# Gated delta rule feeding a folded four-matrix FFN on one core: the first five chunks' work cut into one-engine steps and issued from a single list

## The chip, the cores and the metric

The kernel runs on one core of a Trainium2 chip. The metric is the device time of one execution in microseconds (us). The core has a matrix engine (TensorE, PE in the profile, with its weight loads as PEld), a vector engine (VectorE, DVE), a scalar engine (ScalarE, ACT), a general engine (GpSimd, POOL) and a sequencer that issues DMAs (SyncE, SP). Each engine takes its instructions strictly in the order in which they were written into its queue.

## The reference

For 4 batches and 8 heads, a 48x48 state is carried over 768 tokens; then a multiplicative FFN is applied to the result.

```python
k_n = k / (np.linalg.norm(k, axis=-1, keepdims=True) + 1e-06)
for t in range(S):
    kt, vt, bt = (k_n[:, :, t], v[:, :, t], beta[:, :, t, None])
    y[:, :, t] = np.einsum('bhd,bhde->bhe', q[:, :, t], state)
    v_old = np.einsum('bhde,bhd->bhe', state, kt)
    state = state + bt[:, :, :, None] * np.einsum('bhd,bhe->bhde', kt, vt - v_old)
...
x = np.ascontiguousarray(attn_out.transpose(0, 2, 1, 3)).reshape(B * S, H * D)
a = x @ w1
b = x @ w2
h = a * b @ w3
return (h @ w_out).astype(np.float32)
```

q, k, v and beta are float32; w1, w2 (384x1024), w3 (1024x1024) and w_out (1024x384) arrive as float64.

## The kernel before

**The recurrence.** The 768 tokens are cut into 12 chunks of 64. For chunk m: `scores(m)` multiplies K by (K, Q) on TensorE and leaves U (scaled, DVE) and PT (masked). U goes to DRAM in 32x32 blocks (`to_blocks`), and for each pair of chunks j `inverse(j)` loads it back as Ub and solves 31 dependent steps on DVE, two operations each (L304, L309). The result Vb goes through DRAM into TT (`from_blocks`); `corner(m)` completes the 64x64 inverse on TensorE, and `chain(m)` does the three products with the state S and the outputs, which ACT copies into xT, the FFN's input.

**The weights.** All float64 weights come in 36 pieces: 8 of w_out (384 KB each), 16 of w3 and 12 of w1 and w2 (512 KB each). A piece is loaded into one of five `raw` buffers and converted (`convert`) by two ACT operations (L470, L471), two DVE operations (L473, L476) and one POOL addition (L479). A buffer is free for the next load when the POOL addition is done; the load of the next piece is written right after it (`converts`). The w3 pieces are transposed on TensorE (L514), and w3 times w_out is computed once, in eight parts (`fold(jc)`, L521, each in two halves), as w34. w_out lies in the space of w2, so w2 can't be converted before the last fold.

**The FFN.** For every pair of chunks u: eight `ab` units (L543, three matmuls with w1 and three with w2, then ACT's copy and DVE's product) and four `o` units (L558, eight matmuls with w34 and the store).

**The order.** Up to half of the second inverse the order is written out by hand, and `in_text_order` ties every engine to it; behind that point (`tc.issue_after`) a scheduler orders the rest by priority and readiness, from the same text order. In the hand-written part a `convert` issues all of its ACT, DVE and POOL operations at one place, and a `transpose_w3` and a `fold` follow the two conversions that they need.

Of the kernel before, what the change touches and what calls it, by code (L numbers as in the profile page):

```python
# [30 lines left out]

@with_exitstack
def kernel(
# [46 lines left out]
    turns = {}  # L82
# [71 lines left out]
    def load_k(m, dma):  # L154
        ktoks[m] = load_tok(k, m, dma, "ktok", 4)

    def load_v(m, dma):
        vtoks[m] = load_tok(v, m, dma, "vtok", 2)

    def load_perm(m, dma):  # L160
        for src, dst in ((k, kperm), (q, qperm)):
            for z in range(2):
                for j in range(2):
                    nd = min(BS, D - BS * j)
                    for tb in range(2):
                        t0 = C * m + BS * tb
                        dma(  # L167
# [6 lines left out]
                        )  # L174

# [6 lines left out]
    def squares(j):  # L182
        sums[j] = ss = small.tile([P, 2, NR, H], FP32, name="ss")
        for cc in range(2):
            kt = ktoks[2 * j + cc]
            for r in range(NR):
                sq = in_turn(work, [P, H, D], "sq", 1, "sq")
                pool.tensor_tensor(out=sq[:], in0=kt[:, r], in1=kt[:, r], op=ALU.mult)
                dve.tensor_reduce(out=ss[:, cc, r], in_=sq[:], axis=AX.X, op=ALU.add)
                yield  # L190
    def norms(j):
        ss = sums.pop(j)
        seed = small.tile([P, 2, NR, H], U32, name="seed")
# [5 lines left out]
        for _ in range(3):  # L199
            t = small.tile([P, 2, NR, H], FP32, name="nt", bufs=3)  # L200
# [4 lines left out]
            rn = small.tile([P, 2, NR, H], FP32, name="nr", bufs=3)  # L205
# [14 lines left out]
        ns[j], ws[j] = n, w  # L220

# [29 lines left out]
    def scores(m, transposed=None):  # L251
        Us[m] = U = in_turn(work, [P, NR, H, C], "U", 2, "U")
        PTs[m] = PT = in_turn(work, [P, NR, H, C], "PT", 3, "PT")
        w = scale_of(ws, m)
        for r in range(NR):
            if transposed:
                transposed(m, r)
            KQ = KQs[m, r]
            ps = two_banks()
            for h in range(H):  # L260
                for z in range(2):
# [5 lines left out]
                    )  # L267
            psv = ps[:].rearrange("p a (h j t) -> p (a h) j t", h=4, j=2)
            dve.tensor_tensor(  # L269
                out=U[:, r], in0=psv[:, :, 0, :],  # L270
                in1=w[:, r].unsqueeze(2).to_broadcast([P, H, C]), op=ALU.mult,
            )
            dve.tensor_tensor(
                out=PT[:, r], in0=psv[:, :, 1, :],
                in1=smask[:].unsqueeze(1).to_broadcast([P, H, C]), op=ALU.mult,
            )
# [6 lines left out]
    def to_blocks(m, dma):  # L283
        j = m // 2
        if m % 2 == 0:
            Uds[j] = dram.tile([P, BS, BS], FP32, tag="Ud", name="Ud")
        for x in range(4):
            dma(
                out=Uds[j][:].rearrange(blocks, x=4, r=NR, h=H)[m % 2, x],
                in_=Us[m][quarter(x), :, :, quarter(x % 2)].rearrange("s r h t -> s (r h) t"),  # L290
            )

    def inverse(j, dma):
        U = work.tile([P, BS, BS], FP32, tag="Ub", name="Ub", bufs=1)
# [16 lines left out]
        Vds[j] = dram.tile([P, BS, BS], FP32, tag="Vd", name="Vd")  # L311
        dma(out=Vds[j][:], in_=V[:])

    def from_blocks(m, dma):
        for x in range(4):
            dma(
                out=TTs[m % 2][quarter(x), :, :, quarter(x % 2)].rearrange("s r h t -> s (r h) t"),
                in_=Vds[m // 2][:].rearrange(blocks, x=4, r=NR, h=H)[m % 2, x],
            )


    def corner(m):
        TT, U = TTs[m % 2], Us.pop(m)
# [6 lines left out]
        ps = psT.tile([P, NR, H, BS], FP32, tag="t", name="ps_t")  # L330
        for r in range(NR):
            for h in range(H):
                for z in range(2):
                    pe.matmul(  # L334
                        ps[quarter(2 * z + 1), r, h, :], lhsT=U[quarter(2 * z), r, h, BS:C],
                        rhs=T11[quarter(2 * z), r, h, :], start=True, stop=True,
                    )
        for z in range(2):
# [3 lines left out]
        ps = psT.tile([P, NR, H, BS], FP32, tag="t", name="ps_t")  # L342
        for r in range(NR):
            for h in range(H):
                for z in range(2):
# [12 lines left out]
    def chain(c):  # L358
        w = scale_of(ws, c)
        TT, PT, kt = TTs[c % 2], PTs.pop(c), ktoks.pop(c)  # L360
        KQ = [KQs.pop((c, r)) for r in range(NR)]
        nv = vtoks.pop(c)
        for r in range(NR):
# [3 lines left out]
            )  # L367

# [10 lines left out]
        if c == 0:  # L379
            R = nv  # L380
        else:
            R = work.tile([P, NR, H, D], FP32, tag="R", name="R", bufs=1)
            ps = products(
                lambda r, h, z: KQ[r][feat(z), h, 0, :], lambda r, h, z: St[feat(z), r, h, :], C
            )
            dve.tensor_tensor(out=R[:], in0=nv[:], in1=ps, op=ALU.subtract)
# [4 lines left out]
        X = in_turn(work, [P, NR, H, D], "X", 2, "X")  # L391
# [389 lines left out]
```

## Time and profile before

| | us |
|---|---|
| median of 3 runs (758.71 to 760.46) | 758.8 |
| the profiled execution's own time | 758.51 |
| its span (first to last instruction) | 756.8 |
| TensorE matmul busy in the span | 645.0 (85%) |
| VectorE, ScalarE, GpSimd busy | 351.8, 156.8, 97.5 |
| DMA moved in the span | 55.60 MB |

The span is what the engines' records cover; 1.7 us lie around it. Busy time of TensorE counts a matmul longer when the granted clock is low, so a busy engine is not one that works at full speed. The first FFN matmul starts at 215.64 us of the span.

### The profile page before, as it was taken

What the parts mean: (1) busy time and instruction counts of PE and PEld (TensorE: products, weight loads), DVE (VectorE), ACT (ScalarE), POOL (GpSimd) and SP (SyncE); (2) the same over time, 40 slices, a digit from 0 to 9 for tenths busy, and PEclk for the clock granted to TensorE, in tenths of its full rate; (3) what the DMA queues carried; (4) which work ended last, traced back from release to release, by engine and by line L of the source; (5) the groups of instructions that cost most, each with busy time, mean ns of one, the idle gap of its engine ahead of it and who ended that gap; (6) DMA issues with size and microseconds to landing.
All of it is one profiled execution on the core that took longest, in us unless ns stands there. A gap on an engine that the chain in (4) does not pass through costs nothing.

```text
span 756.8 us, 17007 instructions
## 1 busy us (share of the span) xinstructions
PE 645.0 (85%) x7372; PEld 400.3 (53%) x7372; DVE 351.8 (46%) x768; ACT 156.8 (21%) x277; POOL 97.5 (13%) x110
## 2 busy tenths in 40 slices
PE   5524577578848999879998999999999999999998
PEld 5512334466613367644667547575476645655444
DVE  2877532331468923478325862369442492200110
ACT  3522223322242022010210113111130112211010
POOL 4331221211154100021000100002000000000000
PEclk9756677675779999999999999999999999999999
DMA  9584551151289053451433432334413402000001
GB/s 193 142 207 128 108 133 56 44 97 29 55 180 127 1 91 54 110 83 34 62 64 86 93 65 36 69 84 83 86 22 55 96 11 57 3 22 32 0 1 42
DMA packets 201834, 55.60 MB, mean 73 GB/s; under 512 B 191968, under 2 KB 195040, under 8 KB 201760
## 3 DMA queue, kind: packets, MB, share of 16 engines
q1 hardware_dynamic: 197600, 53.74, 34.6%
q10 hardware_dynamic: 4160, 0.79, 0.7%
q8 instruction: 58, 0.95, 0.5%
q14 instruction: 16, 0.13, 0.1%
HBM read 42.30 MB, written 11.01 MB: 70 GB/s over the span
## 4 chain that ended last, share of the span: by engine, by line
PE 66%; DVE 13%; issue 4%; DMA 3%; SPq 2%; POOL 2%; ACT 1%; POOLq 0%; DVEq 0%; ACTq 0%
PE ps_f L543 24%; PE ps_f L558 15%; PE ps_w L375 7%; PE ps_w L262 6%; PE ps_f L521 6%; DVE Vb L309 4%; DVE tb L304 4%; PE ps_t L347 2%; PE ps_t L334 2%; DMA raw<-in_moe_w_dram 1%; PE ps_w L425 1%; PE ps_w L420 1%; SPq L167 1%; PE ps_f L514 1%; POOL w L479 1%
## 5 line engine op out<-in xcount | busy, mean ns | idle before, releaser
L543 PE MATMUL ps_f<-xT,w1s 128*128 128x512 f32 x288 | 138.8, 614 | 16.5 <-DMA xT<-xT 11.2
L543 PE MATMUL ps_f<-xT,w2s 128*128 128x512 f32 x288 | 135.3, 601 | 4.8 <-POOL w2s L479 3.9
L558 PE MATMUL ps_f<-w,ab 128*128 128x384 f32 x384 | 128.3, 490 | 0.0
L543 PEld LDWEIGHTS ps_f<-xT,w1s 128*128 128x128 f32 x288 | 54.2, 195 | 83.7 <-issue 60.3
L558 PEld LDWEIGHTS ps_f<-w,ab 128*128 128x128 f32 x384 | 71.9, 190 | 49.6 <-issue 3.0
L543 PEld LDWEIGHTS ps_f<-xT,w2s 128*128 128x128 f32 x288 | 53.8, 191 | 70.1 <-issue 62.1
L553 DVE TENSOR_TENSOR ab<-a,ps_f 128x512 f32<-128x512 f32 x48 | 32.8, 683 | 122.5 <-PE ps_f L543 122.4
L304 DVE TENSOR_TENSOR tb<-Vb,Ub 128x31 f32<-128x31 f32 (+15 forms) x186 | 72.8, 392 | 9.4 <-DMA Ub<-Ud 4.9
L309 DVE TENSOR_TENSOR Vb<-Vb,tb 128x31 f32<-128x31 f32 (+15 forms) x186 | 72.4, 389 | 4.7
L262 PE MATMUL ps_w<-KQ 48*64 48x128 f32 x768 | 57.2, 314 | 16.3 <-DVE KQ L234 11.4
L550 ACT COPY a<-ps_f 128x512 f32<-128x512 f32 x48 | 28.0, 586 | 205.2 <-PE ps_f L543 205.1
L262 PEld LDWEIGHTS ps_w<-KQ 48*64 48x64 f32 x768 | 52.9, 159 | 19.8 <-issue 15.2
L514 PE MATMUL ps_f<-ident,w 128*128 128x128 f32 x64 | 17.3, 424 | 52.3 <-POOL w L479 52.3
L521 PE MATMUL ps_f<-w2s,w3T 128*128 128x384 f32 x128 | 55.4, 593 | 0.0
L364 POOL TENSOR_TENSOR vtok<-vtok,n 128x384 f32<-128x384 f32 x24 | 19.8, 849 | 226.3 <-DMA vtok<-in_v_dram 166.6
L269 DVE TENSOR_TENSOR U<-ps_w,w 128x512 f32<-128x512 f32 x24 | 16.5, 686 | 66.5 <-PE ps_w L262 66.5
L436 ACT COPY xT<-ps_w 48x512 f32<-48x512 f32 x48 | 27.9, 580 | 76.7 <-PE ps_w L425 76.2
L514 PEld LDWEIGHTS ps_f<-ident,w 128*128 128x128 f32 x64 | 11.2, 212 | 58.9 <-POOL w L479 58.6
L521 PEld LDWEIGHTS ps_f<-w2s,w3T 128*128 128x128 f32 x128 | 29.5, 240 | 20.6 <-issue 10.8
L563 ACT COPY osb<-ps_f 128x384 f32<-128x384 f32 x24 | 11.5, 479 | 126.6 <-PE ps_f L558 116.2
L479 POOL TENSOR_TENSOR w<-w,raw 128x512 uint32<-128x512 uint32 x16 | 20.7, 1291 | 116.7 <-DVE w L476 106.1
L393 DVE TENSOR_TENSOR X<-ps_w,w 128x384 f32<-128x384 f32 x24 | 12.3, 553 | 42.5 <-PE ps_w L375 42.5
(78 smaller groups left out, 628.6 us busy)
## 6 DMA issues: line engine op xcount, KB each, us to landing
raw<-in_moe_w_dram SPq DMA_DIRECT2D x16, 512.0 KB, 5.0
vtok<-in_v_dram SPq DMA_DIRECT2D x24, 192.0 KB, 4.0
raw<-in_moe_w_dram SPq DMA_DIRECT2D x24, 192.0 KB, 4.1
out_dram<-osb SPq DMA_DIRECT2D x24, 192.0 KB, 1.9
ktok<-in_k_dram SPq DMA_DIRECT2D x22, 192.0 KB, 4.5
raw<-in_moe_w_out_dram SPq DMA_DIRECT2D x8, 384.0 KB, 6.4
Ud<-U SPq DMA_DIRECT2D x48, 64.0 KB, 1.9
Ub<-Ud SPq DMA_DIRECT2D x6, 512.0 KB, 4.6
```

Of the source, the lines that this page charges most:

```text
L262: pe.matmul(ps[half(z), h // 4, 128 * (h % 4) : 128 * (h % 4) + 128], lhsT=KQ[feat(z), h, 0, :], rhs=KQ[feat(z), h].rearrange("p j t -> p ...
L304: dve.tensor_tensor(out=tv, in0=V[:, 0 : s + 1, s : s + 1].to_broadcast([P, s + 1, n]), in1=U[:, s, s + 1 : BS].unsqueeze(1).to_broadcast( ...
L309: dve.tensor_tensor(out=o, in0=o, in1=tv, op=ALU.subtract)
L375: pe.matmul(o, lhsT=lhs(r, h, z), rhs=rhs(r, h, z), start=True, stop=True)
L436: act.copy(out=xT[f, :, NR * z : NR * z + NR, cc, :].rearrange("p a r t -> p r a t"), in_=pyv[f, z],)
L479: pool.tensor_tensor(out=au, in0=au, in1=lo, op=ALU.add)
L514: pe.transpose(ps[:, x, :], w3[:, x * P : (x + 1) * P], ident[:])
L521: pe.matmul(ps[:, 0:DM], lhsT=w3Ts[jc, kc // 4][:, kc % 4 * P : kc % 4 * P + P], rhs=wo[:, kc], start=(kc == 0), stop=(kc == KF - 1),)
L543: pe.matmul(ps[:], lhsT=w[:, m, js], rhs=cur["x"][:, m].rearrange("p b c t -> p (b c t)"), start=(m == 0), stop=(m == KM - 1),)
L550: act.copy(out=a[:], in_=pair[0][:])
L553: dve.tensor_tensor(out=t[:], in0=a[:], in1=pair[1][:], op=ALU.mult)
L558: pe.matmul(ps[:, 0:DM], lhsT=cur["ab"][jc][:, b * P : (b + 1) * P], rhs=w34[:, jc, :], start=(jc == 0), stop=(jc == KF - 1),)
```

## The change

All parts (`scores`, `inverse`, `corner`, `chain`, the new `outputs` and `scaled_v`, `piece` in place of `load_weight` and `convert`, `transpose_w3`, `fold`, `ab`, `o`, the loads) become generators that yield after the work of each single engine. A string of 551 names, `ORDER`, says which part takes its next step; it ends behind the fourth chunk's outputs, the sixth chunk's scores (s5) and the whole third inverse. The tail behind it is as before, from chunk 4 on. In the names, P0 to P7 are w_out pieces, P8 to P23 w3 pieces, P24 to P29 w1, P30 to P35 w2; t is a transposition of a w3 piece, f a fold, s scores, u to_blocks, V an inverse, e a corner, n the scaled v, c a chain, y outputs, a0x a unit `ab`, o0x a unit `o`, k, q, v, p loads, K and Q transposed k and q, g and N the norms.

Beside the order, three things change: the first inverse (V0) works in PSUM, in one of the two two-bank buffers, which is held for it (`held`), with ACT copying in and out; PT of the first two chunks is copied by ACT and masked by POOL in place of one DVE operation; and q, k, v, w_out and w3 pieces are loaded in another order.

```diff
+ORDER = """
+P10 P2 k0 K00 g0 q0 P2 P2 P2 P10 P10 P10 K01 g0 g0 K00 P1 P1 k1 K10 P1 beta K01 K01 K00 beta
...
     def in_turn(pool, shape, tag, n, name, dt=FP32):
 
-        i = turns[tag] = (turns.get(tag, -1) + 1) % n
-        return pool.tile(shape, dt, tag=f"{tag}{i}", name=name, bufs=1)
+        i = turns.get(tag, -1)
+        while True:
+            i = turns[tag] = (i + 1) % n
+            if (tag, i) not in held:
+                return pool.tile(shape, dt, tag=f"{tag}{i}", name=name, bufs=1)
...
+            if m < 2:
+                act.copy(out=PT, in_=psv[:, :, 1, :])
+                yield
+                pool.tensor_tensor(out=PT, in0=PT, in1=mask, op=ALU.mult)
+            else:
+                dve.tensor_tensor(out=PT, in0=psv[:, :, 1, :], in1=mask, op=ALU.mult)
+            yield
...
+        V = Vb
+        if j == 0:
+
+            V = two_banks().rearrange("p a (s t) -> p (a s) t", t=BS)
+            held.add(("w", turns["w"]))
+            for i in range(0, BS, BS // 2):
+                act.copy(out=V[:, i : i + BS // 2], in_=Vb[:, i : i + BS // 2])
+                yield
...
+        if j == 0:
+            for i in range(0, BS, BS // 2):
+                act.copy(out=Vb[:, i : i + BS // 2], in_=V[:, i : i + BS // 2])
+                yield
+            held.clear()
...
-    def convert():
-        dst, raw = pieces.pop(0)
+        yield
         dst = dst()
-        n = dst.shape[1]
         lo, hi = raw[:, 0:n, 0], raw[:, 0:n, 1]
+        du = dst.bitcast(U32)
 
         act.activation(out=dst, in_=hi.bitcast(FP32), func=ACTF.Abs, scale=2.0**-112)
         act.activation(out=lo, in_=lo, func=ACTF.Copy, scale=2.0**-29)
...
+        yield
+        dve.tensor_scalar(out=du, in0=du, scalar1=3, scalar2=None, op0=ALU.logical_shift_left)
+        dve.scalar_tensor_tensor(
+            out=du, in0=hi, scalar=0x80000000, in1=du, op0=ALU.bitwise_and, op1=ALU.bitwise_or
         )
...
+        yield
+        pool.tensor_tensor(out=du, in0=du, in1=lo, op=ALU.add)
+        yield
...
+    for name in ORDER.split():
+        step(name)
     in_text_order()
```

What this does to three queues is shown as the rows of the built programs, before and after. TensorE between the second chunk's scores and the second fold, before (L514 transposes a w3 piece, L521 is a fold; x8 is a whole fold, x4 half of one):

```order
L262 MATMUL ps_w<-KQ 64x128 x64
L514 MATMUL ps_f<-ident,w_487 128x128 x4
L514 MATMUL ps_f<-ident,w_495 128x128 x4
L514 MATMUL ps_f<-ident,w_526 128x128 x4
L514 MATMUL ps_f<-ident,w_552 128x128 x4
L521 MATMUL ps_f<-w2s,w3T 128x384 x8
L514 MATMUL ps_f<-ident,w_602 128x128 x4
L514 MATMUL ps_f<-ident,w_628 128x128 x4
L521 MATMUL ps_f<-w2s,w3T 128x384 x8
```

and after (L578 transposes, L587 folds, L389 is the first corner's first product):

```order
L288 MATMUL ps_w<-KQ 64x128 x32
L578 MATMUL ps_f<-ident,w_140 128x128 x4
L578 MATMUL ps_f<-ident,w_450 128x128 x4
L578 MATMUL ps_f<-ident,w_217 128x128 x4
L578 MATMUL ps_f<-ident,w_503 128x128 x4
L578 MATMUL ps_f<-ident,w_526 128x128 x4
L578 MATMUL ps_f<-ident,w_495 128x128 x4
L587 MATMUL ps_f<-w2s,w3T 128x384 x16
L578 MATMUL ps_f<-ident,w_643 128x128 x4
L578 MATMUL ps_f<-ident,w_591 128x128 x4
L587 MATMUL ps_f<-w2s,w3T 128x384 x16
L578 MATMUL ps_f<-ident,w_706 128x128 x4
```

Six transpositions now stand ahead of the first fold, and folds follow each other two at a time with no transposition between them. On DVE, in the first inverse (tb and Vb steps are L304 and L309), each conversion of a w3 piece (L473, L476) stands before:

```order
L309 TENSOR_TENSOR Vb<-Vb,tb 128x12x20
L473 TENSOR_SCALAR w_602<-w_602 128x512
L476 SCALAR_TENSOR_TENSOR w_602<-raw,w_602 128x512
L304 TENSOR_TENSOR tb<-Vb,Ub 128x247
```

and the stretch of the same steps after (L350 and L355 are the steps, L538 and L539 the conversions; w2s at 384 columns is a w_out piece):

```order
L355 TENSOR_TENSOR ps_w<-ps_w,tb 128x10x22
L538 TENSOR_SCALAR w_591<-w_591 128x512
L539 SCALAR_TENSOR_TENSOR w_591<-raw,w_591 128x512
L538 TENSOR_SCALAR w2s<-w2s 128x384
L539 SCALAR_TENSOR_TENSOR w2s<-raw,w2s 128x384
L538 TENSOR_SCALAR w2s<-w2s 128x384
L539 SCALAR_TENSOR_TENSOR w2s<-raw,w2s 128x384
L538 TENSOR_SCALAR w2s<-w2s 128x384
L539 SCALAR_TENSOR_TENSOR w2s<-raw,w2s 128x384
L350 TENSOR_TENSOR tb<-ps_w,Ub 128x231
```

One w3 piece and the last three w_out pieces stand inside the inverse, which now reads and writes PSUM (ps_w). On SP, the DMA queue from the first inverse's input (Ub) on, before:

```order
L295 DMA Ub<-Ud 128x1024
L459 DMA raw<-in_moe_w_dram 128x1024 x3
L144 DMA ktok<-in_k_dram 64x16x48 x4
L144 DMA vtok<-in_v_dram 64x16x48 x2
L459 DMA raw<-in_moe_w_dram 128x1024 x4
L167 DMA kperm_96<-in_k_dram 32x16x32 x2
```

and after:

```order
L336 DMA Ub<-Ud 128x1024
L527 DMA raw<-in_moe_w_out_dram 128x768 x2
L527 DMA raw<-in_moe_w_dram 128x1024
L171 DMA ktok<-in_k_dram 64x16x48 x2
L527 DMA raw<-in_moe_w_out_dram 128x768 x2
L527 DMA raw<-in_moe_w_dram 128x1024
L527 DMA raw<-in_moe_w_dram 48x1024
```

Before, all w_out pieces were loaded ahead of Ub, and w1 came behind all of w3; now four w_out pieces follow Ub, six w3 pieces and one w1 piece stand ahead of it, and w1 pieces are mixed with w3 pieces.

## Rows read from the trace of the kernel before

**Rows 1.** Windows: length; busy PE, PEld, DVE, ACT, POOL; PEclk, DMA share, GB/s:

```profile
0.00:215.60 215.60, 131.55 (x1548) 98.32 (x1548) 102.69 (x201) 64.25 (x115) 52.52 (x60) 0.71 0.48 110
...
215.60:258.90 43.30, 35.73 (x73) 14.39 (x73) 33.26 (x69) 9.90 (x17) 15.87 (x15) 0.93 0.68 111
...
258.90:346.80 87.90, 78.09 (x1149) 51.37 (x1149) 47.00 (x111) 14.15 (x25) 8.46 (x10) 0.96 0.40 73
```

**Rows 2.** Who waited for whom: us in total, times, longest:

```profile
POOL w L479 <- DVE w L476: 106.1, 14, 18.9
...
PE ps_f L514 <- POOL w L479: 52.3, 14, 7.5
...
SPq L459 <- POOL w L479: 79.4, 10, 18.4
```

**Rows 3.** Timeline of TensorE: start, us, instruction, idle before it and its releaser:

```profile
73.34 1.11 PE L514 MATMUL ps_f<-ident,w 128*128 128x128 f32 x4 [6.25 <-POOL w L479]
...
74.25 7.52 PE L521 MATMUL ps_f<-w2s,w3T 128*128 128x384 f32 x16
...
215.64 4.29 PE L543 MATMUL ps_f<-xT,w1s 128*128 128x512 f32 x6 [7.31 <-DMA xT<-xT]
```

**Rows 4.** Two windows of 20 us, columns as in Rows 1:

```profile
0.00:20.00 20.00, 11.37 (x283) 10.82 (x285) 6.32 (x12) 8.28 (x14) 9.30 (x19) 1.00 0.92 184
...
40.00:60.00 20.00, 8.69 (x26) 5.58 (x27) 13.65 (x31) 4.56 (x8) 5.17 (x4) 0.55 0.88 205
```

**Rows 5.** Timeline of SP and DVE around the first inverse:

```profile
44.78 0.34 SPq L295 DMA_DIRECT2D Ub<-Ud  x1
...
48.07 0.77 DVE L304 TENSOR_TENSOR tb<-Vb,Ub 128x31 f32<-128x31 f32 x1 [0.69 <-DMA Ub<-Ud]
...
90.02 0.21 DVE L309 TENSOR_TENSOR Vb<-Vb,tb 128x31 f32<-128x31 f32 x1
...
97.73 4.04 SPq L316 DMA_DIRECT2D TT<-Vd  x8
```

**Rows 6.** Timeline of DVE and POOL, one conversion inside the first inverse:

```profile
68.51 0.42 DVE L309 TENSOR_TENSOR Vb<-Vb,tb 128x256 f32<-128x256 f32 x1
...
70.67 0.42 DVE L473 TENSOR_SCALAR w<-w 128x512 uint32<-128x512 uint32 x1
...
71.13 0.69 DVE L476 SCALAR_TENSOR_TENSOR w<-raw,w 128x512 uint32<-128x512 uint32 x1
...
71.95 1.33 POOL L479 TENSOR_TENSOR w<-w,raw 128x512 uint32<-128x512 uint32 x1 [6.04 <-issue]
...
72.18 1.38 DVE L309 TENSOR_TENSOR Vb<-Vb,tb 128x247 f32<-128x247 f32 x1
```

**Rows 7.** Groups of lines, 0 to 215.6 us: busy us, mean ns:

```profile
L309 DVE TENSOR_TENSOR Vb<-Vb,tb 128x31 f32<-128x31 f32 (+15 forms) x31 | 14.6, 471 | 1.1
...
L304 DVE TENSOR_TENSOR tb<-Vb,Ub 128x31 f32<-128x31 f32 (+15 forms) x31 | 11.1, 360 | 1.6 <-DMA Ub<-Ud 0.7
```

**Rows 8.** Groups of lines, whole span, two DVE operations that read PSUM:

```profile
L269 DVE TENSOR_TENSOR U<-ps_w,w 128x512 f32<-128x512 f32 x24 | 16.5, 686 | 66.5 <-PE ps_w L262 66.5
...
L393 DVE TENSOR_TENSOR X<-ps_w,w 128x384 f32<-128x384 f32 x24 | 12.3, 553 | 42.5 <-PE ps_w L375 42.5
```

**Rows 9.** DMA issues: KB each, median us to landing:

```profile
raw<-in_moe_w_dram SPq DMA_DIRECT2D x16, 512.0 KB, 5.0
...
TT<-Vd SPq DMA_DIRECT2D x48, 64.0 KB, 2.3
```

**Rows 10.** Chain that ended last, TensorE pieces at full clock: start, us, what:

```profile
363.35 1.13 PE ps_t L334 x64
...
398.79 3.64 PE ps_w L262 x64
...
405.77 2.00 PE ps_w L375 x64
...
732.46 20.65 PE ps_f L558 x64
```

More of the change, by code (lines that the diff above doesn't have):

```diff
@@ L367, in chain @@
             )
+            yield
+    def chain(c):
+        TT, nv = TTs[c % 2], vtoks[c]
+        KQ = [KQs[c, r] for r in range(NR)]
         def products(lhs, rhs, rows):
@@ L410, in chain, with outputs @@
             yield
+    def outputs(c):
+        PT, St, X = PTs[c], Ss.get(c), Xs[c]
+        KQ = [KQs[c, r] for r in range(NR)]
         py = two_banks()
@@ new lines, in ab, with o @@
+        yield
+    def o(u, b):
+        ps = bank([P, NT])
+        for jc in range(KF):
+            pe.matmul(
+                ps[:, 0:DM], lhsT=abs_[u, jc][:, b * P : (b + 1) * P], rhs=w34[:, jc, :],
+                start=(jc == 0), stop=(jc == KF - 1),
+            )
+        yield
+        osb = in_turn(ffn, [P, DM], "o", 2, "osb")
+        act.copy(out=osb[:], in_=ps[:, 0:DM])
+        yield
+        t0 = b * S + u * 2 * C
+        sync.dma_start(out=out[t0 : t0 + P, :], in_=osb[:])
+        yield
@@ L629 @@
-    norms(0)
-    for r in range(NR):
-        by_tensor(1, r, 1, qs[1])
-        converts(1)
-    for m in range(2):
-        first = scores(m)
-        for _ in range(2):
-            next(first)
-            converts(1)
-        to_blocks(m, sp)
-    V = inverse(0, sp)
-    next(V)
-    converts(3)
-    transpose_w3(0)
-    load_k(2, sp)
-    load_k(3, sp)
-    load_v(0, sp)
-    folds = [fold(jc) for jc in range(KF)]
-    corners = [corner(0), corner(1)]
-    chains = [chain(0), chain(1)]
-    later = [scores(2, by_vector), scores(3, by_vector)]
@@ L702 @@
[L702 to L715 removed]
+        yield
+        ps = bank([P, NCH, NR * H])
+        for c in range(NCH):
+            pe.transpose(
+                ps[:, c, :], beta_fm[:, c].rearrange("p z t -> p (z t)"),
+                ident[0 : 2 * H, 0 : 2 * H],
+            )
@@ new lines, in betas_ @@
+        yield
+        dve.tensor_copy(
+            out=beta_tok[:].rearrange("p c r h -> p c (r h)"), in_=ps[:, :, 0 : NR * H]
+        )
+        yield
+    parts = {"beta": betas_}
+    for m in range(NCH):
+        parts[f"k{m}"] = lambda m=m: load_k(m, act.dma_start if m == 0 else sync.dma_start)
+        parts[f"v{m}"] = lambda m=m: load_v(m)
+        parts[f"p{m}"] = lambda m=m: load_perm(m)
+        parts[f"s{m}"] = lambda m=m: scores(m)
+        parts[f"u{m}"] = lambda m=m: to_blocks(m)
+        parts[f"e{m}"] = lambda m=m: corner(m)
+        parts[f"n{m}"] = lambda m=m: scaled_v(m)
+        parts[f"c{m}"] = lambda m=m: chain(m)
+        parts[f"y{m}"] = lambda m=m: outputs(m)
@@ L716, with step, finish @@
+    running = {}
+    def step(name):
+        if name not in running:
+            running[name] = parts[name]()
+        next(running[name], None)
+    def finish(*names):
+        for name in names:
+            if name not in running:
+                running[name] = parts[name]()
+            for _ in running[name]:
+                pass
+    for name in ORDER.split():
+        step(name)
     in_text_order()
+    last = [i for i in nc.cur_bb.bb.instructions if i.engine == mybir.EngineType.SP][-1]
@@ L719, in emit @@
+    units = [f"a1{jc}" for jc in range(KF)] + [f"o1{b}" for b in range(B)]
     def emit(n):
[L720 to L739 removed]
+        finish(*units[:n])
+        del units[:n]
```

431 lines of the change are left out of this document (179 added, 252 removed).

## The prediction, made before the run

> **What bounds the kernel now.** I read four views: the windows for a cut into stages, the waits for what stands behind the idle time, the timelines for the pace of one conversion and of the first inverse, and the chain for full-clock prices. The windows [rows 1] show two kernels in one. Up to 215.6 us, where the first FFN matmul starts [rows 3], TensorE is busy 131.6 us at a mean granted clock of 0.71 and idle for 84; behind that it is nearly always busy: idle 7.6 of 43.3 and 9.8 of 87.9 us in the next two stretches. No other engine fills the front: DVE is busy 102.7, ACT 64.3, POOL 52.5 of 215.6 us, and DMA moves 110 GB/s, where it moved 184 and 205 in its best stretches [rows 4].
>
> So what bounds the front is a round trip. A w3 piece needs ACT, then DVE (0.42 + 0.69 us), then POOL (1.33) [rows 6], then TensorE, and the hand-written order issues the next piece behind the previous fold's copy and between steps of the inverse. The waits [rows 2] show each link: POOL waits 106.1 us for DVE's half of a conversion, TensorE 52.3 us for POOL's addition in front of its transpositions, and SP 79.4 us for POOL to free a load buffer. Each pause also costs speed: a fold of 16 records behind an idle 6.25 us took 7.52 us [rows 3], while at full clock (64 records of the same shape in 20.65 us, 0.323 each [rows 10]) it would be 5.16.
>
> **The change, part by part.** Nothing on TensorE is added or removed; the change moves the start of the FFN. I call that start F (215.6 before) and work out the new one, first along the engines, then by bytes.
>
> *First inverse, start.* DMA sizes follow from shapes: a w_out piece 0.393 MB, a w1, w2 or w3 piece 0.524 [rows 9], a q, k or v tile (64 tokens x 32 heads x 48 x 4 bytes) 0.393, U's blocks of one chunk 0.262, Ub, Vd or two chunks' TT 0.524. Ahead of Ub in the new queue stand six w3, one w1 and four w_out pieces, five q and k tiles, half a K/Q load (0.393), beta and U's blocks of two chunks: 8.22 MB. I take 190 GB/s, between the two best stretches and nearer the first, which has small rows: 43 us, plus 2.3 for the last blocks to land [rows 9], plus the 3.3 from Ub's issue to the first step before [rows 5]: 49 us, against 48.07. Nothing is won here, though four w_out pieces fewer are loaded by then.
>
> *First inverse, run.* It took 25.7 us of DVE time [rows 7], of which some 3.5 are steps that ran beside a POOL addition: 1.38 where a like step takes 0.42 [rows 6]. With V in PSUM I expect 2 x 11.1 = 22.2 us, 0.72 for each pair. Inside it now stand w_out pieces whose last (P7) comes 11.23 MB into the queue: 59 + 2.3 = 61.4, ACT's part about 1.1 like DVE's, then three pieces on DVE, to 66. Behind them 21 of 31 steps (15), two more pieces (2.2) and a sum of squares: the inverse ends at about 84, against 90.2 [rows 5]. ACT copies V back (two operations of 512 columns, 1.4 by DVE's price for 512, [rows 8]); then as before 7.5 us from the inverse's end to the issue of TT [rows 5], 2.3 to land and a transposition of 0.7 (bounded by a 512-column operation, [rows 8]): the first corner starts at 96, late by no more than the queue's backlog.
>
> *Folds.* All w_out is converted at about 68. From there TensorE has eight half folds at 2.58 and three transpositions (1.11 at low clock [rows 3], about 0.55 at full): 22.3, plus 2.4 to come to speed (7.52 less 5.16), so it is done at 93 and is not what the corner waits for. Conversions are ahead because each step of a piece is issued where its engine reaches it.
>
> *Corner to F.* TensorE's list from the first corner to the first FFN matmul, at full-clock prices [rows 10]: four corner products at 1.13, both halves of two scores at 3.64 for each, seven transpositions at 0.55, eight products or outputs of 64 records at up to 2.00 and the second outputs counted double (18 in all with it), seven half folds at 2.58: 4.5 + 7.3 + 3.9 + 18 + 18.1 = 52. I add 4 for DVE's parts between products. F = 96 + 52 + 4 = 152.
>
> *By bytes.* 33 of 36 weight pieces (16.25), twelve q, k, v tiles, two K/Q loads, four U, two Ub, Vd and TT, beta: 25.8 MB come ahead of xT's shift. At 190 GB/s 136 us, 2 to start, 10 in which SP stands at Vd (P21 is issued some 10 us ahead of the inverse's end, and P18, P15 and P27 queue behind it), and 4 for the shift, on which TensorE waits 7.31 before [rows 3]: 152 as well. At 205 GB/s this is 142, and the engine path shrinks to 144; at 160 it is 177. I take 152.
>
> *Behind F.* Before, 756.8 - 215.6 = 541.2 us. One product of the third chunk (2.0) moves ahead of F. Of the 17.4 us idle in the two stretches [rows 1] I take back 5, since the second and third inverse stand among eight FFN units with their chunks' scores ahead: 534. Bounds: 527 if 12 come back, 546 if the new mix loses 7. PT by ACT and POOL takes four DVE operations of 0.68 away and gives ACT four copies and POOL four products; both are over 70% idle in the front, so it costs nothing there, and if POOL were full it would be 4 x 1.33 = 5 us. The single-step generators add no instruction.
>
> Sum: 152 + 534 = 686 of span, plus 1.7 around it: 688 us. The profiled execution (758.51) stands 0.3 under the median, so no correction.
>
> [...] Two operations that read PSUM take 686 ns at 512 columns and 553 at 384 [rows 8]: 1.04 ns a column and 154 ns fixed; the step of 256 columns all in SBUF takes 0.42 [rows 6], which leaves the same 154 or so. By the trace PSUM costs nothing. [...] The rows decide, so I keep 688.
>
> **Rivals.**
> 1. *Transfers stay slow* (0.16). The rows for it: the front's mean is 110 GB/s. Against: SP then stood still 79.4 us for buffers [rows 2]. At 115 to 150 us more waiting or 130 to 160 GB/s: F between 177 and 214, 713 to 750 us.
> 2. *Slower than before, by the DMA queue* (0.05). SP is one queue, and P18 and all behind it stand behind Vd's wait. If the queue moves no more than 110 GB/s: 25.8 MB take 235, with the 16 above F = 250, 786 us. It decides at F = 223, which is 125 GB/s. Against it speak both windows [rows 4], in which the queue had work.
> 3. *No change: the clock stays low* (0.04). The granted clock is 0.71 over the front [rows 1]. [...] Against: the fold in [rows 3] came to full speed inside its 7.52 us, and folds now follow each other. [...]
> 4. *DVE becomes the bound just behind F* (0.05, 700 us). The products of the first `ab` units now stand behind the whole second inverse on DVE, and TensorE can run six products (15.5 us) until it has no PSUM bank. By bytes the second Ub lands near 138; 25 us of steps and four other operations end it at 168, as TensorE runs dry: each us later costs one, up to 12.
> 5. *Better than worked out* (0.08): F near 140 and the idle time behind it gone, under 664.
>
> **How the numbers follow.** My forecast, 688 with a range of its own of 666 to 712, has 0.62. The range for 8 in 10 leaves out rival 5 and the upper part of rivals 1 and 2 and 3: 664 to 722, from F = 142 with none of the 17.4 us of idle left behind it (522) to F = 174 with 546. A measurement of this kernel can tell about 0.3% (2.3 us) from no change. Faster takes the forecast, rivals 1, 4 and 5: 0.91; no change 0.04; slower 0.05.
>
> **What would show it.** Right: the first w1 matmul between 140 and 165 us; the first inverse ends near 84, with no step beside a POOL addition three times as long as its neighbours; folds in pairs of about 5.2 us and a granted clock over 0.9 from 75 us on; DMA at 170 GB/s or more over the first 90 us; TensorE's wait for POOL ahead of transpositions far under 52.3; 500 to 515 us of busy TensorE behind F, as before. Wrong: SP waiting long at Ub or Vd with idle DMA engines, ACT or DVE standing at a piece not yet landed while work behind it is ready (each queue is strictly in order, so one late piece holds all), or `ab` products that wait for the second inverse.

## The result and the profile after

The changed kernel takes 690.24 us (median of 4 runs, 685.44 to 692.04) where the kernel before takes 758.75 beside it: a ratio of 0.908, 95% interval 0.903 to 0.914. The forecast was 688 with 664 to 722. The profiled execution took 688.65 us, its span is 686.9. A second set of six runs, beside the experiments below, gave a median of 693.1 and a ratio of 0.912 (0.909 to 0.916); where a variant is compared with the changed kernel, these two ratios are the yardstick. A ratio is a kernel's time over that of the kernel before, measured in the same set.

The windows show where the 69.9 us of span went. Columns as in [rows 1]; the cut is at the first FFN matmul:

```profile
0.00:156.20 156.20, 110.76 (x1548) 84.56 (x1549) 111.80 (x231) 70.34 (x127) 62.74 (x66) 0.82 0.77 168
156.20:687.00 530.80, 512.03 (x5824) 302.00 (x5824) 239.30 (x534) 89.99 (x159) 40.98 (x48) 0.99 0.29 55
```

The FFN starts 59.4 us earlier than before [rows 1]; what stands behind it is shorter by 10.5 us (541.2 to 530.7). In the front the same 1548 matmuls are busy for 110.8 us instead of 131.6, because the mean granted clock is 0.82 instead of 0.71, and TensorE is idle for 45.4 us instead of 84. So about a third of the front's gain is speed and two thirds are pauses that are gone. Behind the start the busy time is nearly that of before, and idle time fell from 27.8 to 18.8 us.

The waits, as in [rows 2]; the last four lines are SP's own, up to 156.2 us:

```profile
POOL w L543 <- DVE w L539: 21.4, 4, 10.8
PE ps_f L578 <- POOL w L543: 15.0, 2, 10.5
PE ps_f L607 <- DMA xT<-xT: 7.3, 2, 4.0
...
SPq L527 <- POOL w2s L543: 8.8, 3, 8.1
SPq L188 <- DVE KQ L259: 8.5, 1, 8.5
SPq L324 <- DVE U L298: 4.9, 1, 4.9
SPq L527 <- POOL w L543: 4.9, 3, 3.6
```

For the w3 pieces all three links of the old round trip shrank: POOL on DVE from 106.1 to 21.4, TensorE on POOL from 52.3 to 15.0, SP on POOL from 79.4 to 4.9. What SP still waits for in the front are load buffers behind w_out pieces (8.8 us, 18.0 before), DVE's transposition of K and Q, which frees the buffers kperm and qperm for the next load (8.5), and U (4.9, 13.5 before). Hold on to the last two: they come back below.

TensorE's timeline, start, duration, instruction, and idle time before it with its releaser:

```profile
60.98 12.30 PE L587 MATMUL ps_f<-w2s,w3T 128*128 128x384 f32 x32 [5.65 <-ACT w3T L581]
...
74.70 10.59 PE L587 MATMUL ps_f<-w2s,w3T 128*128 128x384 f32 x32 [0.55 <-ACT w L594]
89.83 1.11 PE L578 MATMUL ps_f<-ident,w 128*128 128x128 f32 x4 [4.54 <-POOL w L543]
91.62 4.28 PE L587 MATMUL ps_f<-w2s,w3T 128*128 128x384 f32 x8 [0.68 <-ACT w3T L581]
95.83 1.20 PE L389 MATMUL ps_t<-T,U 32*32 32x32 f32 x64
...
150.18 2.07 PE L435 MATMUL ps_w<-S,KQ 48*64 48x48 f32 x64
156.21 9.54 PE L607 MATMUL ps_f<-xT,w1s 128*128 128x512 f32 x18 [3.97 <-DMA xT<-xT]
```

Where one fold of 16 records took 7.52 us behind a pause [rows 3], two folds of together 32 records now take 12.30 behind one and 10.59 when they follow each other. And the last line has the same releaser as in [rows 3]: the FFN still starts when the shift of xT lands. In the profiled execution of the second set the corner starts at 93.9 us and the FFN at 156.3, but the part behind takes 536.5 us instead of 530.7, with TensorE busy 518.4 instead of 512.0 at a mean granted clock of 0.97 instead of 0.99. So a difference of under 6 us behind the start, between single executions, shows nothing.

### The profile page after: what moved, and what is told of

The parts are those of the page before. It is cut to its first block, busy times and chain, and to the rows that moved or that the text cites. A ratio compares the mean times of both kernels' runs of the same rounds, so it can differ in the third digit from the quotient of the medians.

```text
span 686.9 us, 16999 instructions
## 1 busy us (share of the span) xinstructions
PE 622.8 (91%) x7372; PEld 386.6 (56%) x7372; DVE 351.1 (51%) x764; ACT 160.3 (23%) x285; POOL 103.7 (15%) x114
## 4 chain that ended last, share of the span: by engine, by line
PE 68%; DVE 13%; DMA 6%; SPq 6%; issue 3%; POOL 2%; ACT 1%; ACTq 0%; DVEq 0%; POOLq 0%
PE ps_f L607 31%; PE ps_f L627 15%; PE ps_w L435 7%; PE ps_w L288 5%; DVE Vb L355 4%; DVE tb L350 4%; SPq L188 4%; PE ps_f L587 2%; PE ps_t L403 2%; PE ps_t L389 2%; PE ps_w L486 1%; PE ps_w L491 1%; DMA raw<-in_moe_w_dram 1%; DMA raw<-in_moe_w_out_dram 1%; DMA Ud<-U 1%
## 5 line engine op out<-in xcount | busy, mean ns | idle before, releaser
L350 DVE TENSOR_TENSOR tb<-Vb,Ub 128x31 f32<-128x31 f32 (+15 forms) x155 | 57.6, 371 | 6.1 <-DMA Ub<-Ud 1.8
L355 DVE TENSOR_TENSOR Vb<-Vb,tb 128x31 f32<-128x31 f32 (+15 forms) x155 | 58.1, 375 | 4.5
L288 PE MATMUL ps_w<-KQ 48*64 48x128 f32 x768 | 51.2, 289 | 4.3 <-DVE KQ L259 2.2
L587 PE MATMUL ps_f<-w2s,w3T 128*128 128x384 f32 x128 | 47.3, 525 | 6.9 <-ACT w3T L581 6.3
L288 PEld LDWEIGHTS ps_w<-KQ 48*64 48x64 f32 x768 | 46.5, 144 | 9.6 <-issue 5.9
L298 DVE TENSOR_TENSOR U<-ps_w,wt 128x512 f32<-128x512 f32 x24 | 16.4, 688 | 56.3 <-PE ps_w L288 55.9
L587 PEld LDWEIGHTS ps_f<-w2s,w3T 128*128 128x128 f32 x128 | 25.6, 206 | 25.2 <-ACT w3T L581 7.1
L454 DVE TENSOR_TENSOR X<-ps_w,wt 128x384 f32<-128x384 f32 x24 | 12.3, 553 | 42.3 <-PE ps_w L435 42.2
L210 POOL TENSOR_TENSOR sq<-ktok 128x384 f32<-128x384 f32 x24 | 21.4, 891 | 63.2 <-DVE ss L212 32.9
L578 PE MATMUL ps_f<-ident,w 128*128 128x128 f32 x64 | 12.8, 354 | 17.7 <-POOL w L543 15.0
L435 PEld LDWEIGHTS ps_w<-R,TT 64*64 64x64 f32 x704 | 22.4, 135 | 9.9 <-issue 4.6
## 6 DMA issues: line engine op xcount, KB each, us to landing
raw<-in_moe_w_dram SPq DMA_DIRECT2D x16, 512.0 KB, 5.3
Ub<-Ud SPq DMA_DIRECT2D x6, 512.0 KB, 4.1
```

Of the source, the lines that this page charges most:

```text
L288: pe.matmul(ps[half(z), h // 4, 128 * (h % 4) : 128 * (h % 4) + 128], lhsT=KQ[feat(z), h, 0, :], rhs=KQ[feat(z), h].rearrange("p j t -> p ...
L350: dve.tensor_tensor(out=tv, in0=V[:, 0 : s + 1, s : s + 1].to_broadcast([P, s + 1, n]), in1=U[:, s, s + 1 : BS].unsqueeze(1).to_broadcast( ...
L355: dve.tensor_tensor(out=o, in0=o, in1=tv, op=ALU.subtract)
L435: pe.matmul(o, lhsT=lhs(r, h, z), rhs=rhs(r, h, z), start=True, stop=True)
L587: pe.matmul(ps[:, 0:DM], lhsT=w3Ts[jc, kc // 4][:, kc % 4 * P : kc % 4 * P + P], rhs=wo[:, kc], start=(kc == 0), stop=(kc == KF - 1),)
```

## The experiments

The theory: conversions run ahead, so TensorE finds its folds ready; what ends the front then is TensorE's own list or the bytes. The rivals: the new order of loads and chunks does it, and splitting adds little; the first inverse in PSUM does it; or a queue sets the end of the front.

**1. All steps of a conversion issued together, late.** A change in how the list of names is issued:

```
-        next(running[name], None)
+        seen[name] = seen.get(name, 0) + 1
+        if name[0] == "P" and seen[name] in (2, 3, 4):
+            for _ in range(3 if seen[name] == 4 else 0):
+                next(running[name], None)
+        else:
+            next(running[name], None)
```

> All three steps of a weight piece's conversion (ACT, DVE, POOL) are issued together, at the place where the changed kernel issues the last of them; the loads and everything else keep their places. Theory (the gain comes from each engine's step standing where that engine reaches it, so that conversions run ahead): a fold again waits for a chain of ACT, DVE and POOL, 2 to 3 us for each piece that TensorE needs next; TensorE waits for POOL 30 us or more ahead of transpositions (15.0 in the changed kernel, 52.3 before), the first FFN matmul comes at 175 to 215 us (156.2 in the changed kernel) and the time is 710 to 750 us. Rival (the order of loads, folds and chunks does it, and splitting a piece adds little): first FFN matmul within 5 us of 156, time 685 to 697.

730.2 us, ratio 0.959 (0.952 to 0.966): a bit over half of the gain is lost. Its windows, and its timeline of TensorE:

```profile
0.00:177.40 177.40, 118.38 (x1548) 88.71 (x1548) 114.55 (x240) 68.88 (x125) 61.82 (x67) 0.81 0.68 148
177.40:724.80 547.40, 519.78 (x5824) 307.07 (x5824) 232.90 (x525) 91.02 (x161) 39.33 (x47) 0.97 0.28 54
```

```profile
102.26 1.20 PE L389 MATMUL ps_t<-T,U 32*32 32x32 f32 x64
...
154.79 1.12 PE L578 MATMUL ps_f<-ident,w 128*128 128x128 f32 x4 [4.72 <-POOL w L543]
...
177.47 9.52 PE L607 MATMUL ps_f<-xT,w1s 128*128 128x512 f32 x18 [7.48 <-DMA xT<-xT]
191.38 6.83 PE L607 MATMUL ps_f<-xT,w2s 128*128 128x512 f32 x12 [4.38 <-POOL w2s L543]
```

The start of the FFN comes 21.3 us later, as the theory had it, and another 11 to 17 us are lost behind it (547.4 against 530.7 and 536.5), which it had not: the w2 pieces are now late too (last line). But TensorE's wait for POOL ahead of transpositions is 16.8 us in all, not over 30: the lateness spreads over all engines and does not show as one wait.

**2. All steps together, early.** DVE's and POOL's parts are issued where ACT's stands (the change is shown against run 1):

```
-            for _ in range(3 if seen[name] == 4 else 0):
+            for _ in range(3 if seen[name] == 2 else 0):
```

> The three steps of a conversion are issued together again, but at the place of the first (ACT's). Theory: ACT is not late here, but DVE stands at a piece whose ACT part is not done while steps of the inverse behind it are ready: the first inverse ends 5 to 15 us later than 82.0, the first FFN matmul comes at 160 to 175, time 695 to 710; POOL loses nothing. Rival (what counts is that conversions come early at all, not that DVE and POOL have places of their own): first FFN matmul at 154 to 158, time 685 to 693, and the late variant alone is slow.

697.29 us, ratio 0.916 (0.909 to 0.923), above the changed kernel's two ratios by 0.004 and 0.008, with intervals that overlap. The inverse ends at 88.95, 6.9 us later than in the changed kernel. Its first step (the last line) comes at 55.83 instead of 47.2: two w_out pieces now stand ahead of it on DVE, and at one of them DVE waits 3.27 us for ACT's part:

```profile
53.00 0.36 DVE L538 TENSOR_SCALAR w2s<-w2s 128x384 uint32<-128x384 uint32 x1 [3.27 <-ACT w2s L535]
...
55.83 0.18 DVE L350 TENSOR_TENSOR tb<-ps_w,Ub 128x31 f32<-128x31 f32 x1
```

The FFN starts at 160.6 instead of 156.2. So what run 1 gave back is owed to ACT's and DVE's parts being issued late. That the three steps have three places of their own is worth 3 to 6 us by the ratios, which these runs hardly tell from nothing.

**3. The first inverse in SBUF.** V stays in `Vb`, without ACT's four copies:

```
-        if j == 0:
+        if j < 0:
             V = two_banks().rearrange("p a (s t) -> p (a s) t", t=BS)
...
-        if j == 0:
+        if j < 0:
             for i in range(0, BS, BS // 2):
                 act.copy(out=Vb[:, i : i + BS // 2], in_=V[:, i : i + BS // 2])
```

> The first inverse works in SBUF as before (the four copies by ACT are left out); all else as changed. By the prediction's rows: some steps run beside POOL's additions and take 1.4 instead of 0.42 us, 3.5 us in all, ACT's four copies (1.4 us on the path) are saved: first inverse ends at 83 to 86 instead of 82.0, time 688 to 694. [...]

699.29 us, ratio 0.920 (0.914 to 0.926): worse than the 688 to 694 expected. The trace showed that the edit had done more than it meant. The inverse's generator has four steps fewer, so each later name in the list stood for a later step, and the write of Vd moved two places ahead in SP's queue:

```profile
68.79 9.23 SPq L188 DMA_DIRECT2D qperm<-in_q_dram  x8
83.86 0.34 SPq L363 DMA_DIRECT2D Vd<-Vb  x1
84.24 1.51 SPq L171 DMA_DIRECT2D vtok<-in_v_dram  x2
85.85 0.97 SPq L527 DMA_DIRECT2D raw<-in_moe_w_dram  x1
```

SP stood at Vd from 78.0 to 83.9 us with v's load and a weight load behind it, which need nothing of Vd. The first corner came at 102.83 and the FFN at 164.3.

**4. The same with every place kept.** Empty steps stand where ACT's copies were:

```
             for i in range(0, BS, BS // 2):
-                act.copy(out=V[:, i : i + BS // 2], in_=Vb[:, i : i + BS // 2])
                 yield
...
             for i in range(0, BS, BS // 2):
-                act.copy(out=Vb[:, i : i + BS // 2], in_=V[:, i : i + BS // 2])
                 yield
```

> The first inverse in SBUF again, now with every other step left at its place: the four places of ACT's copies stay empty, so the write of Vd keeps its place in SP's queue behind v's second load. In the run before, the write of Vd had come two places earlier, and SP stood at it from 78.0 to 83.9 us with v's load and a weight load behind it. Theory (that queue was the whole loss, the clash with POOL costs little): inverse ends at 82 to 85, first corner at 95 to 98, first FFN matmul at 156 to 159, time within 3 us of the changed kernel. Rival (steps beside POOL are the loss): first corner at 100 or later, first FFN matmul at 161 or later, 5 to 9 us over the changed kernel.

692.02 us, ratio 0.909 (0.905 to 0.913), beside the changed kernel's 0.912 in the same set: no difference in time. The two inverses by group, first in SBUF and then, in the changed kernel, in PSUM (line numbers of the two programs differ by 3; busy us, mean ns):

```profile
L352 DVE TENSOR_TENSOR Vb<-Vb,tb 128x31 f32<-128x31 f32 (+15 forms) x31 | 16.9, 546 | 1.1
L347 DVE TENSOR_TENSOR tb<-Vb,Ub 128x31 f32<-128x31 f32 (+15 forms) x31 | 13.5, 436 | 0.9
```

```profile
L355 DVE TENSOR_TENSOR ps_w<-ps_w,tb 128x31 f32<-128x31 f32 (+15 forms) x31 | 10.8, 349 | 1.1
L350 DVE TENSOR_TENSOR tb<-ps_w,Ub 128x31 f32<-128x31 f32 (+15 forms) x31 | 10.5, 338 | 0.9
```

PSUM makes the inverse 9.1 us shorter on DVE (30.4 to 21.3), and its last step ends at 82.0 instead of 88.0 (82 to 85 were expected for SBUF). The first corner comes 2.8 us earlier (95.83, 98.61), the FFN 2.8 us earlier (156.2, 159.0), and the end, within what these runs tell, not at all.

**5. The first two chunks' masked scores on DVE again.** One operation by DVE in place of ACT's copy and POOL's product.

```
-                act.copy(out=PT, in_=psv[:, :, 1, :])
+                dve.tensor_tensor(out=PT, in0=psv[:, :, 1, :], in1=mask, op=ALU.mult)
                 yield
-                pool.tensor_tensor(out=PT, in0=PT, in1=mask, op=ALU.mult)
```

> The masked scores of the first two chunks are made by DVE in one operation again, not by ACT's copy and POOL's product. Theory (prediction: hidden there, DVE has four operations of 0.69 more ahead of the first inverse, 2.8 us, and the first inverse starts when DVE is through its conversions): the inverse starts at 48 to 50 instead of 47.2 and the time is 690 to 694, at most 3 us more. Rival (POOL's and ACT's parts are late themselves and delay conversions): time 684 to 689.

691.76 us, ratio 0.909 (0.904 to 0.914); the inverse starts at 47.44. No difference: this part of the change costs and brings nothing that these runs can tell.

**6. v's load ahead of qperm's.** One name moves in the list:

```
-v0 n0 n0 p2 f2 V0 V0 V0 V0 V0 P14 V0 V0 V0 v1 n1 n1
+v0 n0 n0 v1 p2 f2 V0 V0 V0 V0 V0 P14 V0 V0 V0 n1 n1
```

The chain that it aims at, in the changed kernel, is this (SP, then POOL, then DVE):

```profile
68.42 10.20 SPq L188 DMA_DIRECT2D qperm<-in_q_dram  x8
78.67 1.32 SPq L171 DMA_DIRECT2D vtok<-in_v_dram  x2
...
83.47 1.62 POOL L419 TENSOR_TENSOR vtok<-vtok,n 128x384 f32<-128x384 f32 x2 [5.41 <-DMA vtok<-in_v_dram]
...
88.05 3.15 POOL L543 TENSOR_TENSOR w<-w,raw 128x512 uint32<-128x512 uint32 x2
...
91.67 0.70 DVE L380 STREAM_TRANSPOSE T<-TT 128x512 f32<-128x512 f32 x1
```

The corner's operand is there at 92.4, but its matmuls start at 95.83, because TensorE has a half fold ahead of them, which waits for a transposition, the transposition for POOL's addition, and POOL for v. Beside it ran the changed kernel itself:

> The changed kernel once more, as the measure for the runs beside it: first FFN matmul at 156 us, first corner at 96, 685 to 692 us.

> One load is moved: the second chunk's v goes ahead of the eight small-row loads of qperm in SP's queue. In the changed kernel SP needs 10.2 us to issue qperm, v lands at 83.5, POOL's products of v wait for it 5.4 us, the addition of piece P20 stands behind them, its transposition comes at 89.83 behind 4.54 us of idle TensorE, and the half fold behind it ends as the first corner's matmuls start, 3.5 us after their operand is there. Theory (POOL's place in this queue holds the corner): transposition at 85 to 87, first corner at 92 to 93.5, first FFN matmul 2 to 4 us earlier, time 2 to 4 us lower. Rival (TensorE's list, not the corner's start, sets the rest, or qperm lands too late for DVE): no change, within 1 us.

685.95 us, ratio 0.903 (0.900 to 0.906), against 693.1 and 0.912 (0.909 to 0.916) beside it: 7.1 us faster, and all six executions (683.89 to 689.28) lie below all six of the changed kernel (690.17 to 697.07). Against the first set's 0.908 it would be 4 us. Its timeline of TensorE:

```profile
83.88 0.66 PE L578 MATMUL ps_f<-ident,w 128*128 128x128 f32 x4 [0.59 <-POOL w L543]
...
90.39 1.20 PE L389 MATMUL ps_t<-T,U 32*32 32x32 f32 x64
...
151.38 9.59 PE L607 MATMUL ps_f<-xT,w1s 128*128 128x512 f32 x18 [4.33 <-DMA xT<-xT]
```

The wait for POOL is 0.59 instead of 4.54 us, the corner starts at 90.4 and the FFN at 151.4. The theory had 2 to 4 us for it; the start alone came 4.8 us earlier.

**7. The same, and xT's shift earlier.** Three runs bring the shift (the last `y1`) forward, on top of run 6. The first puts it ahead of the last two w2 pieces' loads and of v's and k's in SP's queue, the second ahead of v's and k's alone, the third at the place of the first but into ACT's queue:

```
-y1 V1 y1 f4 f4 f4 g2 V1 c2 P33 P33 v3 P33 k5 P34 P34 P35 P35 P35 V1 V1 g2 V1 V1 P34 P35 g2 V1 V1 V1 y1
+y1 V1 y1 y1 f4 f4 f4 g2 V1 c2 P33 P33 v3 P33 k5 P34 P34 P35 P35 P35 V1 V1 g2 V1 V1 P34 P35 g2 V1 V1 V1
...
+y1 V1 y1 f4 f4 f4 g2 V1 c2 P33 P33 P33 P34 P34 P35 y1 v3 k5 P35 P35 V1 V1 g2 V1 V1 P34 P35 g2 V1 V1 V1
...
-                    sync.dma_start(out=xT[g : g + 16, j], in_=xT[s : s + 16, NP - 1])
+                    (act if u == 0 else sync).dma_start(out=xT[g : g + 16, j], in_=xT[s : s + 16, NP - 1])
```

> The same move, and the shift of xT is issued right behind the four ACT copies that feed it, ahead of P35, v and k loads in SP's queue. In the changed kernel it stands behind them until 151.8, though its data are there at 147.3, and TensorE waits 3.97 us. Theory: both waits go; first FFN matmul at 149 to 151 (the product of the third chunk ahead of it then ends the wait), time 5 to 8 us under the changed kernel. Rival (bytes set the start: the DMA engines are 77% busy in this stretch): first FFN matmul at 154 or later, time 0 to 3 us lower.

> Both moves again, but the shift of xT now stands behind the last two w2 loads (P33 and P35) in SP's queue and ahead of v's and k's next loads. In the run before, SP stood at the shift from 137.8 to 144.0 us with those w2 loads behind it, and TensorE waited 7.74 us for POOL's w2 conversion at 157.4. Theory: the shift is issued at 143 to 145, first FFN matmul at 148 to 150, no wait over 2 us for w2; time 2 to 4 us under the variant with v's load alone moved, ratio to before 0.895 to 0.902. Rival (the start of the FFN no longer sets the end: what it gains is lost to DVE or to the second inverse behind it): ratio 0.902 to 0.906.

> The variant with v's load alone moved, and the six transfers of the first xT shift issued by ACT, right behind its copies that feed them, instead of by SP behind four weight, v and k loads; SP's other transfers keep their order. Theory (SP's order, not bytes and not TensorE's list, holds the start of the FFN): first FFN matmul at 146 to 149 instead of 151.4, with no wait for the shift over 1.5 us. If the start sets the end, time 681 to 684, ratio 0.896 to 0.901. Rival (behind the start the w2 pieces and DVE's products come no earlier, so the gain is given back, as in the two runs that moved the shift inside SP's queue): ratio 0.901 to 0.906.

695.07, 686.5 and 687.86 us; ratios 0.914 (0.911 to 0.917), 0.904 (0.900 to 0.908) and 0.904 (0.899 to 0.910). The FFN starts at 149.4, 149.7 and 148.3 instead of run 6's 151.4, as expected, and none of it is seen at the end: by its ratio the first is slower than run 6 (0.903, 0.900 to 0.906), the other two are level with it. A gain of 2 to 3 us could hide in these intervals. For the third, TensorE:

```profile
148.29 7.99 PE L607 MATMUL ps_f<-xT,w1s 128*128 128x512 f32 x18
162.00 7.26 PE L607 MATMUL ps_f<-xT,w2s 128*128 128x512 f32 x12 [5.72 <-POOL w2s L543]
```

The wait of 4.33 us ahead of the start is gone, and one of 5.72 for POOL's part of a w2 conversion has come up 8 us behind the start; in the first two runs it is 7.74 and 2.56, in run 6 nothing. The conversion itself comes later: POOL is through with it at 165.1, 160.2 and 162.0 us, in run 6 at 158.2. In the first run the w2 loads stand behind the shift; in the third SP, with w2 loads next in its queue, stands 5.9 us that the profile puts down to the shift. Behind the start these kernels need 540.3, 533.0 and 537.3 us, and run 6 531.0; since two executions of the changed kernel differ by 5.8 there, only the first is clearly longer. The last two ratios lie where the rival had them, with what the start gains not seen at the end, and no kernel here is faster than that of run 6.

**8. More bytes.** The w3 pieces P15 to P18 are also copied, right behind their own loads, into memory that nothing reads.

```
+            if more:
+                scratch = dram.tile([P, 2 * CW], U32, tag=f"x{len(extra)}", name="extra", bufs=1)
...
+                sync.dma_start(out=scratch[:], in_=src.bitcast(U32))
```

> The changed kernel with four more transfers: the w3 pieces P15 to P18 are also copied, 0.524 MB each, into memory that nothing reads, right behind their own loads in SP's queue, between the end of the first inverse and the start of the FFN. 2.1 MB at the front's 168 GB/s are 12.5 us. If bytes set the start (the prediction's second way to 152 us): first FFN matmul at 166 to 170, time 699 to 705. If TensorE's list and the waits in its queues do: at most 4 us later, time 690 to 697.

701.47 us, ratio 0.924 (0.919 to 0.928), 8.7 us over the changed kernel's 0.912. The profiled execution was the fastest of its four (694.7; the others 700.5 to 705.1); in it the FFN starts at 159.20, 3.0 us later. So the time lies in the range of the bytes and the start in that of the other theory: transfers are not free there, but 12.5 us of them moved the start by 3. Up to the start this execution moved 178 GB/s, where the changed kernel moved 168: the 168 were no ceiling. The rest of its loss stands in executions without a profile and stays open.

**9. Less work for TensorE.** Six of the eight products of f3, f4 and f5 are left out.

```
+            if jc in (3, 4, 5) and kc not in (0, KF - 1):
+                if kc == KF // 2 - 1:
+                    yield
+                continue
```

> The changed kernel with six of the eight products left out of each of the folds f3, f4 and f5 (the result differs): some 13 us less TensorE work ahead of the FFN, the same bytes. If TensorE's list sets the start of the FFN: first matmul 8 to 13 us earlier, 143 to 148, and the span about 13 us shorter. If bytes or SP's queue do: first matmul within 3 us of 156, TensorE idle ahead of it for 10 us or more, span at most 5 us shorter.

One execution: 695.84 us, span 694.0. TensorE, and SP ahead of the shift:

```profile
130.03 1.92 PE L403 MATMUL ps_t<-TT,T 32*32 32x32 f32 x64 [5.23 <-ACT T L396]
...
145.92 2.27 PE L435 MATMUL ps_w<-S,KQ 48*64 48x48 f32 x64
158.16 10.34 PE L611 MATMUL ps_f<-xT,w1s 128*128 128x512 f32 x18 [9.97 <-DMA xT<-xT]
```

```profile
136.33 2.73 SPq L324 DMA_DIRECT2D Ud<-U  x4
140.53 0.34 SPq L336 DMA_DIRECT2D Ub<-Ud  x1
...
152.84 3.93 SPq L514 DMA_DIRECT2D xT<-xT  x6
```

TensorE has some 13 us less to do, but is through at 148.2, only 4 us earlier, and then waits 9.97 us: the start did not move forward at all. The rest of the 13 us went into waits and lower speed. Between the first corner and that last wait the longest is in the first line, where TensorE stands for the second corner's T. ACT copies T at 128.8, behind two w1 conversions for whose loads it had waited 6.17 and 1.53 us. In the changed kernel ACT waits 5.61 and 1.30 us for them, copies T at 128.6, and the same product starts at 129.99, behind a whole fold. The fourth chunk's scores behind that wait ran slower, the second half in 3.68 us instead of 1.96, with a mean granted clock of 0.53 from 130 to 136 us, where the changed kernel had 1.00. So this run shows that TensorE's list alone does not set the start; what the list would be worth with these loads earlier, it can't show. SP in the changed kernel:

```profile
102.80 4.82 SPq L188 DMA_DIRECT2D kperm<-in_k_dram  x8
107.72 4.95 SPq L188 DMA_DIRECT2D qperm<-in_q_dram  x8
...
133.85 1.91 SPq L324 DMA_DIRECT2D Ud<-U  x4
138.89 0.34 SPq L336 DMA_DIRECT2D Ub<-Ud  x1
139.28 3.68 SPq L527 DMA_DIRECT2D raw<-in_moe_w_dram  x8
143.48 2.13 SPq L171 DMA_DIRECT2D vtok<-in_v_dram  x2
145.71 2.91 SPq L171 DMA_DIRECT2D ktok<-in_k_dram  x2
148.66 3.04 SPq L527 DMA_DIRECT2D raw<-in_moe_w_dram  x4
151.80 3.75 SPq L514 DMA_DIRECT2D xT<-xT  x6
```

ACT has finished xT at 147.3. SP waits for the fourth chunk's U (whose scores TensorE ends at 133), for its blocks to land, issues Ub, then 16 transfers, and 12.9 us behind Ub the shift. The same 12.9 us lie between the two in the kernel of run 6 (134.22 to 147.10) and 12.3 in run 9. The loads that ACT waits for are in the same queue: SP stands for DVE's KQ from 94.3 to 102.8 us (the 8.5 above), issues the 16 small-row loads of kperm and qperm until 112.7, and only then the next weights. So by these rows SP's queue decides when the FFN starts, through these loads and through the shift. Only the shift's part was tested (run 7), and it is worth 2 to 3 us at the start: in the first and third of run 7 TensorE goes from its list into the FFN without a wait, so there the list ends last.

## Why the prediction was right, step by step

**The first inverse: right.** Ub was issued at 43.2 (45.3: 43 by bytes, 2.3 for the blocks to land), the first step ran at 47.2 (49) and the last ended at 82.0 (84). What held its first step was DVE's conversions ahead of it, not the transfer. The steps in PSUM took 21.3 us (22.2). The size of the clash was wrong: 3.5 us in the kernel before, but 9.1 if V were in SBUF in this order, where POOL adds during the inverse. It mattered little, as run 4 shows.

**The price of PSUM: the rows were right.** They gave an estimated 154 ns fixed for PSUM and SBUF alike, so no cost for reading PSUM. The last step (31 columns, two operations) took 0.19 and 0.20 us in PSUM and 0.20 and 0.21 in SBUF, that of 256 columns 0.42 and 0.43 against 0.42 and 0.42, all without POOL beside them: the same within 0.01 us.

**The first corner at 96: right number, wrong reason.** The operand was there at 92.4, and the step that failed is the one that had TensorE done with its folds at 93 and "not what the corner waits for". It was done at 95.8, because one transposition waited 4.54 us for POOL, and POOL 5.41 us for v behind qperm. The forecast's sum of half folds and transpositions had no wait in it. Run 6 removes most of this one: the corner comes 5.4 us earlier, the end 7.1.

**From the corner to the FFN: 60.4 us, not 56, and for another reason.** TensorE was busy 53.8 of these (52 forecast) and idle for 6.6 (4). The size was right, but the list alone isn't the bound: run 9 shortens it by 13 us and gains nothing at the start. "10 in which SP stands at Vd" was the right kind of wait in the wrong place: SP stands 2.1 us at Vd, 8.5 at KQ and 4.9 at the fourth chunk's U, and the shift waits behind 12.9 us of loads.

**By bytes: 152, measured 156.2, in part by luck.** The forecast's 25.8 MB in 152 us are a mean of 170 GB/s, with its waits; measured are 26.2 MB at a mean of 168. But 12.5 us more of transfers moved the start by only 3 (run 8), so they alone do not set it. The agreement of two sums was no proof of either: neither names the queue that decided, and both came near because the limits lie close together. TensorE is through its list at 152.2, the shift lands at 156.2.

**Behind the FFN's start: 530.7 us, 534 forecast.** 9.0 us of idle time came back, not 5; the busy 512.0 us are inside 500 to 515 (518.4 in the second set's profiled execution are not). Rival 4 did not come: TensorE waited 2.7 us for DVE's products.

**Signs.** Waits for POOL, the start, the inverse's end and the absence of clashes came as said; the second pair of folds took 5.3 us for each (about 5.2), the first, behind a pause, 6.2; DMA moved 184 GB/s over the first 90 us (170 or more). The clock did not: it was to be over 0.9 from 75 us on and had a mean of 0.87 from 80 to 160, with the second chunk's first product, at 118.9 us, taking 3.63 us where the full clock needs 2.00 [rows 10].

**The range.** The lower end, 664, leaves out the 1.7 us around the span that the upper end has; with them it is 666. The measured time is far from either.

**Why it is faster.** "Conversions are ahead because each step of a piece is issued where its engine reaches it" is half the story. Run 1 shows that starting them late gives back a bit over half of the gain, run 2 that the three places as such matter little. The other half, which run 1 keeps, is left to the order of loads, folds and chunks, since PSUM and the masked scores brought nothing measurable (runs 4 and 5); no run here takes that order apart. In the trace of before, the first corner's matmuls start at

```profile
120.16 1.92 PE L334 MATMUL ps_t<-T,U 32*32 32x32 f32 x64
```

behind folds that each wait for POOL, and at 102.26 in run 1, where they are done earlier. That this is the mechanism of the other half is argued, not shown.

## What to carry to other kernels

Where one engine's in-order queue issues every transfer, ask at each place what stands behind a load that waits or that takes long to issue: one load moved past eight small-row transfers was worth about 1%, and a write of Vd moved by two places cost 8 us (run 3 against run 4). When two sums give the same time, take one of them away by experiment before believing either. And a wait taken away in front of a stage is a gain only if the stage's second operand is also early: in three ways to start the FFN 2 to 3 us sooner, TensorE then stood 2.6 to 7.7 us at a w2 conversion 8 us behind the start.

## What the runs showed of the hardware

Steps of the inverse that ran beside a POOL addition took far longer with both operands in SBUF (1.38 us where the same columns take 0.41); with V in PSUM they did not. Two steps of the same 240 columns, in run 4 and in the changed kernel, each while POOL added (63.25 to 64.69 and 71.00 to 72.29 us):

```profile
63.58 1.38 DVE L347 TENSOR_TENSOR tb<-Vb,Ub 128x240 f32<-128x240 f32 x1
```

```profile
71.59 0.41 DVE L350 TENSOR_TENSOR tb<-ps_w,Ub 128x240 f32<-128x240 f32 x1
```

The first had both inputs in SBUF, the second one of them in PSUM. Why the first took longer, these rows do not show. The surprise was how little the 9.1 us were worth: 2.8 at the corner and nothing measurable at the end.
